# Flush of small numbers by a bit mask made on ScalarE, and words loaded three chunks ahead

## The chip, the core and the metric

The kernel runs on one core of a Trainium2 chip. The core has five engines that work through queues of their own, each in order: TensorE (PE; its weight loads are PEld), VectorE (DVE), ScalarE (ACT), GpSimd (POOL) and SyncE (SP), which here only issues transfers. 16 DMA engines carry the transfers between the chip's memory and the on-chip buffers. The metric is the device time of one execution, in microseconds, as the median of the runs.

## The reference

Three parts follow each other: attention over q, k, v (4 batches, 8 heads, 768 positions, 64 numbers a head, a local window and a few global positions), a mixture of eight experts with one expert per token, and a gated unit. All inputs are fp32 except the weights of the gated unit, whose scale makes them float64 on the host:

```
a = softmax(scale * q k^T + bias, masked);  x = a v            # attention, 3072 tokens x 512
h = max(xc[mask] @ w1[e], 0);  y[mask] = gate_w * (h @ w2[e])  # expert e, w1 512 x 1024, w2 1024 x 512
out[do_compute] = xc + y
gate = 1 / (1 + exp(-(x @ w_gate)));  val = x @ w_val          # gated unit, 512 x 1536 each
result = (gate * val) @ w_out                                  # w_out 1536 x 512
```

What the change touches is a preparation of the last part: `w_gate`, `w_val` and `w_out` arrive as pairs of 32-bit words of a float64 each, and have to become fp32 before the gated unit can multiply with them.

## The kernel before

**Stages.** Attention runs up to about 250 us, two first tiles of expert 0 up to 293 us, experts 1 to 7 up to 562 us, one tile of overflow up to 582 us, and the gated unit up to the end. The tokens of an expert are gathered from rows in memory (`x_rows`) and scattered back by GpSimd (lines 818 and 863).

**An expert** (`expert`, line 838) has two layers for 256 tokens. The first layer is four steps `mp` of 24 matmuls (line 849), each followed by a Relu on ScalarE (`hT`, line 853) and a call of `hook1`. The second is 16 matmuls (line 868), with a call of `hook2` after every four. The first layer's weights of the next expert are split meanwhile into a high part on ScalarE and a low part on VectorE (`we`, lines 809 and 810, by `split_next`), and the next expert's tokens are transposed (line 832) and split (lines 835 and 836, by `prep_x`). At an expert's end VectorE forms the results (line 862) and GpSimd scatters them in two transfers (line 863), of which the second waits until the first has landed.

**The conversion** (`convert`, line 1353) turns 36 chunks of 128 x 512 float64 numbers into fp32, between the steps of the experts. `load_words` brings the words (tile `cvwg`, four buffers). ScalarE squares the high words read as fp32 (`cvcg`, line 1349). VectorE shifts the high words by three and cuts them (`cvd`, line 1360), sets the top bits (1362), takes the exponent (`cvbg`, 1364) and multiplies the low words by it (1366). GpSimd adds that (1367), turns the square into 0 or 1 by comparing it with a threshold (1369), and multiplies the number by it (1370), which flushes numbers that are too small to zero. A store on ScalarE's queue (`cv_store`, line 788) writes the chunk to memory, from where the gated unit loads it.

**What sets the order.** The generator `conv_steps` (line 947) is cut into two half steps a chunk, and `hook1` and `hook2` of expert e run as many of them as the table `CSE` says: for experts 2 to 6 two in each of the first three calls and one in each of the other five. The instructions of an engine then run in the order in which the code is written (`manual_schedule`), and an instruction that waits holds everything behind it on its engine. In the first half step of chunk n the words of chunk n + 2 are loaded; in the second half the chunk n - 1 is stored and chunk n + 1 is begun.

Of the kernel before, what the change touches and what calls it, by code (L numbers as in the profile page):

```python
# [9 lines left out]
F32 = mybir.dt.float32  # L10
F32R = mybir.dt.float32r
I32 = mybir.dt.int32
U32 = mybir.dt.uint32
AF = mybir.ActivationFunctionType
ALU = mybir.AluOpType
# [3 lines left out]
P = 128  # L19
# [10 lines left out]
NM = F2 // P  # L30
# [31 lines left out]
def _i32(c):  # L62
    return c - (1 << 32) if c >= (1 << 31) else c
# [3 lines left out]
def attention_moe_glu_kernel(  # L67
# [7 lines left out]
    nc = tc.nc  # L75
    n_global, n_local, g_gate, g_val, g_out = [a.bitcast(I32) for a in (n_global, n_local, g_gate, g_val, g_out)]
    cp = ctx.enter_context(tc.tile_pool(name="cp", bufs=1))
# [8 lines left out]
    wg18 = cp.tile([P, NC, 18], F32R, name="wg18")  # L86
    nw = cp.tile([P, 4], I32, name="nw")
    prm = cp.tile([P, 8], F32, name="prm")
    flag = cp.tile([P, 1], I32, name="flag")
    nl, ng = prm[:, 1:2], prm[:, 0:1]  # L90

# [46 lines left out]
    def load_chunk(n, after=None):  # L138

        if n % 8 > 3:  # L140
            pool, tag = (raw_p, "raw") if n < 6 else (web[0], "web")
        else:
            pool, tag = (raw_p if ring_place(n) > 3 else rawb[0]), "raw"
        t = pool.tile([P, 1024], F32, tag=tag, name=f"raw{n}")
        src = chunk_src(n)
        if after is not None:
            after.memset(t[:, 0:1], 0.0)
        nc.sync.dma_start(t if (n % 8) < 4 else t.rearrange("p (a f) -> p a f", a=2), src)
        if n % 8 > 3:
            chunks[n] = t  # L150
        else:
            raw_q[n] = t
# [9 lines left out]
    with ExitStack() as actx:  # L162
# [482 lines left out]
        n = 0  # L645
        step[0] = 0
        while n < NS + LAG + 4 or side or pend or rgen:
            step[0] = n
            if n < NS:
                G, i, pr = steps[n]  # L650
# [87 lines left out]
    cvp = ctx.enter_context(tc.tile_pool(name="cvp", bufs=2))  # L738
# [5 lines left out]
    def cv_src(n):  # L744

        if n < 2 * NM:
            p, gv, hf = n // 4, n // 2 % 2, n % 2
            c = slice(2 * hf, 2 * hf + 2)
            src = (g_gate, g_val)[gv].rearrange("(c p) f -> p c f", p=P)[:, c, p * 4 * P:(p + 1) * 4 * P]
            return src, wd[2 * p + gv][:, c].rearrange("p c m f -> p (c m f)")  # L750
        m = n - 2 * NM
        return g_out[m * P:(m + 1) * P, :], od[m]

    cvw, cvt = {}, {}

    def cv_load(n):
        if n < 3 * NM:
            cvw[n] = load_words(nc, cvp, f"g{n}", cv_src(n)[0])

    cvi = {}  # L760

    def cv_first(n):

        if n < 3 * NM:
            cvt[n] = cvp.tile([P, 512], F32, tag="cvd", name=f"cvd{n}", bufs=3)
            wr = cvw.pop(n)
            cvi[n] = convert(nc, cvp, f"g{n}", wr, cvt[n])
            next(cvi[n])

    wf, ws = {}, {}  # L770

# [14 lines left out]
    def cv_store(n):  # L786
        if n in cvt:
            nc.scalar.dma_start(cv_src(n)[1], cvt.pop(n))


    with ExitStack() as ectx:
# [23 lines left out]
        def gather(key, cols):  # L815
            t = ep.tile([P, 2, DM], F32, tag="xg", name=f"xg{key}", bufs=3)
            for u, c in enumerate(cols):
                nc.gpsimd.indirect_dma_start(
                    t[:, u, :], None, X, IndirectOffsetOnAxis(ap=c, axis=0))
            xgs[key] = t  # L820

        def prep_x(key, nt, half):
            if half == 0:
                xTs[key] = (xep.tile([P, NC, 2 * P], F32R, tag="xeh", name=f"xeh{key}"),
                            xep.tile([P, NC, 2 * P], F32R, tag="xel", name=f"xel{key}"))
            th, tl = xTs[key]
            x = xgs[key]
            pt = ps_g.tile([P, 2, 2 * P], F32, tag="g", name=f"xe{key}_{half}")
            for a in range(2):
                c = 2 * half + a  # L830
                for u in range(nt):
                    nc.tensor.transpose(pt[:, a, u * P:(u + 1) * P], x[:, u, c * P:(c + 1) * P], ident)
            n = nt * P
            sl = slice(2 * half, 2 * half + 2)
            nc.scalar.activation(th[:, sl, :n], pt[:, :, :n], AF.Copy)
            nc.vector.tensor_tensor(tl[:, sl, :n], pt[:, :, :n], th[:, sl, :n].bitcast(F32), ALU.subtract)  # L836
# [98 lines left out]
        def loads():  # L935
            while nload[0] < 8 * NE + 8 and not hold[0] and free(nload[0]):
                load_chunk(nload[0])
                nload[0] += 1
# [6 lines left out]
                loads()  # L945

        def conv_steps():
            cv_first(0)
            for n in range(3 * NM):
                cv_load(n + 2)  # L950
                next(cvi[n])
                yield
                cv_store(n - 1)
                cv_first(n + 1)
                run(cvi.pop(n))
                yield
            cv_store(3 * NM - 1)

        conv = conv_steps()

        col = lambda t, n: t[:, n:n + 1]
# [18 lines left out]
        def at_a(what):  # L980
            if what == ("product", NC0):
                rt.counts(pr)
                run(rt.ranks(B - 1, pr, Bm))
                run(rt.weights(B - 1))
            if what == ("product", NPA):
                rt.places(px, Bm, 0, NS_)
                rt.static_rows(px, idx, scratch[0])
                gather("0b", [col(idx, NE)])
                gather(1, cols(idx, 1))
                rt.weight_rows(B - 1)  # L990

                load_chunk(8, nc.gpsimd)
                nload[0], hold[0] = 9, False
                loads()
                cv_load(0)
                cv_load(1)
            if what == ("hidden", 1):
                next(ov)
            if what == ("out", 3):
                prep_x("0b", 1, 0)  # L1000
                prep_x("0b", 1, 1)
                rt.places(pq, Bm, NS_, 3 * NS_)
                rt.static_weights(pq, prob_s, scratch[0])

        def at_b(what):
# [8 lines left out]
            if what[0] == "out":  # L1014
                loads()

        expert_tile("0a", 0, pcol0, col(idx, 0), at_a)
        expert_tile("0b", 0, col(prob_s, NE), col(idx, NE), at_b)

# [50 lines left out]
    with ExitStack() as gctx:  # L1070
# [7 lines left out]
        V, A, G = nc.vector, nc.scalar, nc.gpsimd  # L1078
# [217 lines left out]
        n = 0  # L1296
        for s in range(NSTEP):
            g, pk = divmod(s, NM)
# [38 lines left out]
def load_words(nc, pool, key, src):  # L1337
    wr = pool.tile([P, 1024], I32, tag="cvw", name=f"cvw{key}", bufs=4)
    if len(src.shape) == 3:
        nc.sync.dma_start(wr.rearrange("p (a n) -> p a n", a=src.shape[1]), src)  # L1340
    else:
        nc.sync.dma_start(wr, src)
    return wr


def squares(nc, pool, key, wr):

    c = pool.tile([P, 512], F32, tag="cvc", name=f"cvc{key}")
    nc.scalar.activation(c, wr.bitcast(F32).rearrange("p (n w) -> p n w", w=2)[:, :, 1], AF.Square)  # L1349
    return c  # L1350


def convert(nc, pool, key, wr, dst):

    V, G = nc.vector, nc.gpsimd
    lo = wr.bitcast(U32).rearrange("p (n w) -> p n w", w=2)[:, :, 0]
    hi = wr.rearrange("p (n w) -> p n w", w=2)[:, :, 1]
    c = squares(nc, pool, key, wr)

    V.tensor_scalar(dst.bitcast(I32), hi, 3, 0x3FFFFFF8, ALU.logical_shift_left, ALU.bitwise_and)  # L1360
    yield
    V.scalar_tensor_tensor(dst.bitcast(I32), hi, _i32(0xC0000000), dst.bitcast(I32), ALU.bitwise_and, ALU.bitwise_or)
    b = pool.tile([P, 512], F32, tag="cvb", name=f"cvb{key}")
    V.tensor_scalar(b.bitcast(I32), dst.bitcast(I32), _i32(0xFF800000), None, ALU.bitwise_and)
    yield
    V.scalar_tensor_tensor(b, lo, 2.0 ** -52, b, ALU.mult, ALU.mult)
    G.tensor_tensor(dst, dst, b, ALU.add)

    G.tensor_scalar(c, c, (2.0 ** -15 * 1.125) ** 2, None, ALU.is_ge)
    G.tensor_tensor(dst, dst, c, ALU.mult)  # L1370


class Route:
# [243 lines left out]
def run(*steps):  # L1617
    for g in steps:
        for _ in g:
            pass  # L1620
# [185 lines left out]
```

## Time and profile before

| | us |
|---|---|
| median of 3 runs (1156.45 to 1164.44) | 1156.73 |
| profiled execution | 1158.71 |
| its span | 1157.0 |

The rows further below come from that one profiled execution. Times are microseconds from the start of the span, unless ns is said. L863 is line 863 of the kernel. A matmul's or a copy's row reads: output <- inputs, sizes, and how often. "Idle before" is how long the engine had nothing to run, and the name behind the arrow is what ended it. The granted clock of TensorE (PEclk) is 1.00 at full speed; the mean of the whole execution is 0.963.

### The profile page before, as it was taken

What the parts mean: (1) busy time and instruction counts of PE and PEld (TensorE: products, weight loads), DVE (VectorE), ACT (ScalarE), POOL (GpSimd) and SP (SyncE); (2) the same over time, 40 slices, a digit from 0 to 9 for tenths busy, and PEclk for the clock granted to TensorE, in tenths of its full rate; (3) what the DMA queues carried; (4) which work ended last, traced back from release to release, by engine and by line L of the source; (5) the groups of instructions that cost most, each with busy time, mean ns of one, the idle gap of its engine ahead of it and who ended that gap; (6) DMA issues with size and microseconds to landing.
All of it is one profiled execution on the core that took longest, in us unless ns stands there. A gap on an engine that the chain in (4) does not pass through costs nothing. (4 is left out here: it accounts for less than half of the span.)

```text
span 1157.0 us, 16882 instructions
## 1 busy us (share of the span) xinstructions
PE 1057.2 (91%) x5602; PEld 858.9 (74%) x5602; DVE 805.3 (70%) x1657; ACT 529.2 (46%) x963; POOL 600.3 (52%) x595
## 2 busy tenths in 40 slices
PE   7999999889987687686789999999999999999998
PEld 7999999876755365355458888878888878888886
DVE  6778888866566456645488777777767785877753
ACT  5897888653213213222354343454343364434333
POOL 6655656632477776977754555313544531455410
PEclk8999999999998988898999999999999999999999
DMA  9565555426886477557232225442324252323243
GB/s 172 130 159 132 137 132 134 132 76 211 328 290 231 149 293 277 187 219 271 96 116 91 73 90 193 145 146 91 119 73 164 92 200 92 127 73 99 84 143 130
DMA packets 150242, 176.37 MB, mean 152 GB/s; under 512 B 84224, under 2 KB 94208, under 8 KB 150144
## 3 DMA queue, kind: packets, MB, share of 16 engines
q1 hardware_dynamic: 142240, 156.81, 43.7%
q10 hardware_dynamic: 5184, 9.44, 2.1%
q0 software_dynamic: 2720, 8.92, 2.1%
q8 instruction: 48, 0.79, 0.3%
q14 instruction: 50, 0.41, 0.1%
HBM read 133.45 MB, written 36.18 MB: 147 GB/s over the span
## 5 line engine op out<-in xcount | busy, mean ns | idle before, releaser
L1231 PE MATMUL p<-B,wsp 128*128 128x512 f32 x1512 | 364.6, 391 | 4.7 <-DVE cp L1237 2.6
L1231 PEld LDWEIGHTS p<-B,wsp 128*128 128x128 f32 x1512 | 283.6, 188 | 68.6 <-DVE cp L1237 4.4
L1237 DVE TENSOR_TENSOR cp<-p,cp 128x512 f32<-128x512 f32 x252 | 167.9, 684 | 88.6 <-PE p L1231 86.1
L1197 PE MATMUL o<-wos,gt 128*128 128x512 f32 x864 | 219.1, 395 | 4.4 <-DVE gt L1187 2.4
L1197 PEld LDWEIGHTS o<-wos,gt 128*128 128x128 f32 x864 | 163.5, 190 | 40.9 <-DVE gt L1187 3.0
L849 PE MATMUL h<-xeh,we 128*128 128x256 f32 x448 | 100.2, 319 | 39.2 <-DVE we L810 27.4
L1180 POOL TENSOR_TENSOR wos<-wo,wos 128x512 fp32r<-128x512 f32 x36 | 62.3, 1730 | 113.0 <-ACT wos L1179 113.0
L784 POOL TENSOR_TENSOR ws<-w 128x256 f32<-128x256 f32 x72 | 53.4, 741 | 129.5 <-DVE wsp L1158 129.5
L868 PE MATMUL y<-raw,hT 128*128 128x512 f32 x224 | 101.7, 597 | 17.3 <-ACT hT L853 17.3
L849 PEld LDWEIGHTS h<-xeh,we 128*128 128x128 f32 x448 | 80.0, 216 | 48.1 <-DVE we L810 31.5
L400 ACT ACTIVATE p<-t,mn 128x256 f32<-128x256 f32 (+1 forms) x192 | 83.6, 484 | 36.5 <-DVE mn L391 35.9
L1349 ACT ACTIVATE cvcg<-cvwg 128x512 f32<-128x512 f32 x36 | 24.2, 673 | 159.6 <-POOL cvd L1370 159.6
L1244 ACT ACTIVATE sg<-cp 128x512 f32<-128x512 f32 x72 | 45.2, 632 | 112.7 <-DVE cp L1237 112.0
L278 POOL TENSOR_TENSOR ks<-ring,ks 128x384 fp32r<-128x384 f32 x56 | 56.2, 1025 | 61.8 <-DVE ks L277 45.9
L868 PEld LDWEIGHTS y<-raw,hT 128*128 128x128 f32 x224 | 40.4, 190 | 64.1 <-issue 40.7
L1186 ACT ACTIVATE gt<-gm 128x512 fp32r<-128x512 f32 x36 | 22.8, 632 | 141.5 <-DVE gm L1251 141.5
L391 DVE CUSTOM_DVE_ANT_0 t<-s,far 128x256 f32<-128x256 f32 (+1 forms) x192 | 69.0, 397 | 20.5 <-PE s L366 16.7
L366 PE MATMUL s<-ks,qs 128*128 128x256 f32 (+1 forms) x384 | 69.4, 300 | 5.1 <-POOL ks L278 2.7
L849 PE MATMUL h<-xel,we 128*128 128x256 f32 x224 | 69.6, 311 | 2.1 <-DVE xel L836 2.0
L438 PE MATMUL o<-v,pts 128*128 128x65 f32 x384 | 70.4, 275 | 1.1 <-issue 1.1
L1247 POOL TENSOR_TENSOR gm<-cp,sg 128x512 f32<-128x512 f32 x36 | 54.4, 1510 | 30.3 <-DVE cp L1237 30.3
L1360 DVE TENSOR_SCALAR cvd<-cvwg 128x512 int32<-128x512 int32 x36 | 20.3, 564 | 69.0 <-DMA wd<-cvd 31.8
(274 smaller groups left out, 2061.0 us busy)
## 6 DMA issues: line engine op xcount, KB each, us to landing
raw<-in_moe_w_dram SPq DMA_DIRECT2D x68, 512.0 KB, 6.6
w<-wd SPq DMA_DIRECT2D x36, 512.0 KB, 4.6
wo<-od SPq DMA_DIRECT2D x72, 256.0 KB, 3.0
hd<-gm SPq DMA_DIRECT2D x36, 256.0 KB, 2.0
hf<-hd SPq DMA_DIRECT2D x36, 256.0 KB, 3.4
qraw<-in_q_dram SPq DMA_DIRECT2D x32, 192.0 KB, 3.3
kraw<-in_k_dram SPq DMA_DIRECT2D x32, 192.0 KB, 3.6
v<-in_v_dram SPq DMA_DIRECT2D x8, 768.0 KB, 6.3
```

What stands on the lines that cost most here:

```text
L278: nc.gpsimd.tensor_tensor(dst[:, 1], kk[:, a], dst[:, 0].bitcast(F32), ALU.subtract)
L366: nc.tensor.matmul(st[:, a, c0:256], qt[:, a, i * P:(i + 1) * P], kt[:, a, e, k0:(i + 1) * P], start=(e == 0), stop=(e == 1))
L391: nc.vector.tensor_tensor_reduce(o, i0, i1, 2.0 ** -(h0 + 1), 3.0e38, ALU.add, ALU.min, mn[:, a:a + 1])
L400: nc.scalar.activation(p[:, a, c0:], t[:, a, c0:], AF.Exp, bias=mn[:, a:a + 1], scale=-1.0)
L438: nc.tensor.matmul(o[:, hh, :], t[:, a, 1, :], vt[:, hh, i, :], start=(i == 0), stop=True)
L849: nc.tensor.matmul(ph[:, a, :n], chunks[cb + c][:, wl, m * P:(m + 1) * P], xx[:, c, :n], start=(s_ == 0), stop=(s_ == len(seq) - 1))
L868: nc.tensor.matmul(ys[u], hh[:, f % 2, u * P:(u + 1) * P], w[:, (f % 2) * DM:(f % 2 + 1) * DM], start=(f == 0), stop=(f == NF - 1))
L1180: (V if h else G).tensor_tensor(t[:, 1], src, t[:, 0].bitcast(F32), ALU.subtract)
L1197: nc.tensor.matmul(o[u], gt[:, hl, u * P:(u + 1) * P], w[:, wl, :], start=(m == 0 and i == 0), stop=(m == NM - 1 and i == 2))
L1231: nc.tensor.matmul(ps, lhs, Bt[k][:, xl, c], start=i == 0, stop=i == len(seq) - 1)
L1237: V.tensor_tensor(into, ps, t, ALU.add)
L1247: G.tensor_tensor(t, src, sgs.pop((b, h)), ALU.mult)
```

## The change

Three things are changed, in the conversion alone.

- ScalarE makes the flush: after the square come a Sign of the square less a threshold (a column `thr`, set by one memset at the start) and a Relu scaled by just under 2. Where the number is kept, the result's bits are 0x3FFFFFFF; where it is flushed they are 0. VectorE's shift of the high words now takes that as the mask of its bitwise and, in place of the constant, so the exponent taken from it is zero too and the low words add nothing. GpSimd's comparison and multiplication (lines 1369 and 1370) are gone; its addition stays.
- The half steps are cut in another place. The first of chunk n now holds the shift and the top bits, the second the exponent, the low words and GpSimd's addition; the mask of chunk n + 1 is made in the second half of chunk n, behind the store of chunk n - 1.
- The words of chunk n + 3 are loaded in step n, and three chunks ahead of the first step, still into four buffers.

```diff
--- before.py
+++ after.py
@@ -86,6 +86,8 @@
     wg18 = cp.tile([P, NC, 18], F32R, name="wg18")
     nw = cp.tile([P, 4], I32, name="nw")
     prm = cp.tile([P, 8], F32, name="prm")
+    thr = cp.tile([P, 1], F32, name="thr")
+    nc.gpsimd.memset(thr, -(2.0 ** -15 * 1.0625) ** 2)
     flag = cp.tile([P, 1], I32, name="flag")
     nl, ng = prm[:, 1:2], prm[:, 0:1]
 
@@ -757,15 +759,16 @@
         if n < 3 * NM:
             cvw[n] = load_words(nc, cvp, f"g{n}", cv_src(n)[0])
 
-    cvi = {}
-    def cv_first(n):
+    cvk = {}
+    def cv_keep(n):
         if n < 3 * NM:
-            cvt[n] = cvp.tile([P, 512], F32, tag="cvd", name=f"cvd{n}", bufs=3)
-            wr = cvw.pop(n)
-            cvi[n] = convert(nc, cvp, f"g{n}", wr, cvt[n])
-            next(cvi[n])
+            cvk[n] = normal_bits(nc, cvp, f"g{n}", cvw[n], thr)
+    def cv_steps(n):
+        cvt[n] = cvp.tile([P, 512], F32, tag="cvd", name=f"cvd{n}", bufs=3)
+        return convert(nc, cvp, f"g{n}", cvw.pop(n), cvk.pop(n), cvt[n])
 
     wf, ws = {}, {}
 
@@ -945,14 +948,15 @@
                 loads()
 
         def conv_steps():
-            cv_first(0)
+            cv_keep(0)
             for n in range(3 * NM):
-                cv_load(n + 2)
-                next(cvi[n])
+                cv_load(n + 3)
+                it = cv_steps(n)
+                next(it)
                 yield
                 cv_store(n - 1)
-                cv_first(n + 1)
-                run(cvi.pop(n))
+                cv_keep(n + 1)
+                run(it)
                 yield
             cv_store(3 * NM - 1)
 
@@ -992,8 +996,8 @@
                 load_chunk(8, nc.gpsimd)
                 nload[0], hold[0] = 9, False
                 loads()
-                cv_load(0)
-                cv_load(1)
+                for n in range(3):
+                    cv_load(n)
             if what == ("hidden", 1):
                 next(ov)
             if what == ("out", 3):
@@ -1343,31 +1347,30 @@
     return wr
 
 
-def squares(nc, pool, key, wr):
+def normal_bits(nc, pool, key, wr, thr):
 
     c = pool.tile([P, 512], F32, tag="cvc", name=f"cvc{key}")
     nc.scalar.activation(c, wr.bitcast(F32).rearrange("p (n w) -> p n w", w=2)[:, :, 1], AF.Square)
+    nc.scalar.activation(c, c, AF.Sign, bias=thr)
+    nc.scalar.activation(c, c, AF.Relu, scale=2.0 - 2.0 ** -23)
     return c
 
 
-def convert(nc, pool, key, wr, dst):
-    V, G = nc.vector, nc.gpsimd
+def convert(nc, pool, key, wr, keep, dst):
+    V = nc.vector
     lo = wr.bitcast(U32).rearrange("p (n w) -> p n w", w=2)[:, :, 0]
     hi = wr.rearrange("p (n w) -> p n w", w=2)[:, :, 1]
-    c = squares(nc, pool, key, wr)
-    V.tensor_scalar(dst.bitcast(I32), hi, 3, 0x3FFFFFF8, ALU.logical_shift_left, ALU.bitwise_and)
+    V.scalar_tensor_tensor(dst.bitcast(I32), hi, 3, keep.bitcast(I32), ALU.logical_shift_left, ALU.bitwise_and)
+    V.scalar_tensor_tensor(dst.bitcast(I32), hi, _i32(0xC0000000), dst.bitcast(I32), ALU.bitwise_and, ALU.bitwise_or)
     yield
-    V.scalar_tensor_tensor(dst.bitcast(I32), hi, _i32(0xC0000000), dst.bitcast(I32), ALU.bitwise_and, ALU.bitwise_or)
     b = pool.tile([P, 512], F32, tag="cvb", name=f"cvb{key}")
     V.tensor_scalar(b.bitcast(I32), dst.bitcast(I32), _i32(0xFF800000), None, ALU.bitwise_and)
-    yield
     V.scalar_tensor_tensor(b, lo, 2.0 ** -52, b, ALU.mult, ALU.mult)
-    G.tensor_tensor(dst, dst, b, ALU.add)
-    G.tensor_scalar(c, c, (2.0 ** -15 * 1.125) ** 2, None, ALU.is_ge)
-    G.tensor_tensor(dst, dst, c, ALU.mult)
+    nc.gpsimd.tensor_tensor(dst, dst, b, ALU.add)
 
 
 class Route:
```

On ScalarE's queue, here from the first Relu of expert 2 on, with `hT` the hidden layer, `wd` the store of a converted chunk, `cvcg` the square or mask and `we` the weights of expert 3. Before:

```order
L853 ACTIVATE hT_0_7356<-h_0_7331 128x512
L788 DMA wd_6683<-cvd_7280 128x512
L1349 ACTIVATE cvcg_7365<-cvwg_7288 128x512
L853 ACTIVATE hT_1_7397<-h_1_7372 128x512
L788 DMA wd_6684<-cvd_7317 128x512
L1349 ACTIVATE cvcg_7406<-cvwg_7358 128x512
L853 ACTIVATE hT_2_7438<-h_2_7413 128x512
```

With the change:

```order
L856 ACTIVATE hT_0_7360<-h_0_7335 128x512
L791 DMA wd_6685<-cvd_7294 128x512
L1355 ACTIVATE cvcg_7368<-cvwg_7269 128x512
L1356 ACTIVATE cvcg_7368<-cvcg_7368,thr 128x512
L1357 ACTIVATE cvcg_7368<-cvcg_7368 128x512
L856 ACTIVATE hT_1_7401<-h_1_7376 128x512
L791 DMA wd_6686<-cvd_7364 128x512
L1355 ACTIVATE cvcg_7409<-cvwg_7292 128x512
L1356 ACTIVATE cvcg_7409<-cvcg_7409,thr 128x512
L1357 ACTIVATE cvcg_7409<-cvcg_7409 128x512
L856 ACTIVATE hT_2_7442<-h_2_7417 128x512
```

The store still stands ahead of the chunk's first activation and of the next Relu; two activations are added between them.

On GpSimd's queue at the same place in the program, from the two scatters at the end of expert 1 on. Before:

```order
L863 DMA x_rows<-xo_0_7325,idx 3200x512
L863 DMA x_rows<-xo_1_7328,idx 3200x512
L1367 TENSOR_TENSOR cvd_7317<-cvd_7317,cvbg_7361 128x512
L1369 TENSOR_SCALAR cvcg_7318<-cvcg_7318 128x512
L1370 TENSOR_TENSOR cvd_7317<-cvd_7317,cvcg_7318 128x512
L1367 TENSOR_TENSOR cvd_7364<-cvd_7364,cvbg_7402 128x512
L1369 TENSOR_SCALAR cvcg_7365<-cvcg_7365 128x512
L1370 TENSOR_TENSOR cvd_7364<-cvd_7364,cvcg_7365 128x512
```

With the change:

```order
L866 DMA x_rows<-xo_0_7329,idx 3200x512
L866 DMA x_rows<-xo_1_7332,idx 3200x512
L1373 TENSOR_TENSOR cvd_7364<-cvd_7364,cvbg_7372 128x512
L1373 TENSOR_TENSOR cvd_7405<-cvd_7405,cvbg_7413 128x512
L1373 TENSOR_TENSOR cvd_7446<-cvd_7446,cvbg_7454 128x512
L1373 TENSOR_TENSOR cvd_7487<-cvd_7487,cvbg_7515 128x512
```

One operation a chunk is left of three; the first chunk's addition still stands behind the second scatter.

## Rows read from the trace of the kernel before

**Rows 1.** Page: busy times of the engines; chain that ended last: its first piece.

```profile
PE 1057.2 (91%) x5602; PEld 858.9 (74%) x5602; DVE 805.3 (70%) x1657; ACT 529.2 (46%) x963; POOL 600.3 (52%) x595
...
582.64 3.48 PE gx L1107 x30
```

**Rows 2.** Busy times by stretch, experts 1 to 7 (the last row lies before them).

```profile
core 0: us, PE busy (x) PEld busy (x) DVE busy (x) ACT busy (x) POOL busy (x), PEclk, DMA share, GB/s
308.29:340.55 32.26, 26.89 (x138) 18.52 (x137) 22.59 (x28) 9.71 (x14) 21.33 (x15) 1.00 0.82 294
340.55:378.20 37.65, 30.72 (x138) 21.12 (x137) 20.26 (x27) 10.28 (x15) 28.77 (x19) 0.86 0.62 214
378.20:422.46 44.26, 31.28 (x139) 21.40 (x138) 23.38 (x32) 10.86 (x16) 32.05 (x22) 0.85 0.66 242
422.46:460.54 38.08, 30.72 (x139) 20.98 (x138) 21.23 (x28) 10.28 (x15) 28.60 (x19) 0.87 0.64 226
460.54:501.82 41.28, 30.38 (x139) 20.59 (x138) 25.24 (x32) 10.85 (x16) 32.33 (x22) 0.88 0.68 252
501.82:542.39 40.57, 30.51 (x138) 20.78 (x137) 23.13 (x31) 10.18 (x15) 28.96 (x20) 0.87 0.65 234
542.39:561.69 19.30, 14.31 (x38) 6.20 (x37) 9.40 (x13) 4.54 (x8) 18.00 (x13) 1.00 0.15 57
293.70:308.29 14.59, 14.59 (x122) 14.35 (x121) 5.81 (x17) 2.38 (x4) 3.33 (x3) 1.00 1.04 399
```

**Rows 3.** Waits from 280 to 570: who waited for whom, total, times, longest.

```profile
ACT cvcg L1349 <- POOL cvd L1370: 159.6, 32, 14.8
...
PE h L849 <- DVE we L810: 27.4, 16, 3.0
...
POOL x_rows L863 <- DMA x_rows<-xo,idx: 19.0, 3, 7.4
...
PE y L868 <- ACT hT L853: 17.3, 11, 3.2
...
DVE cvd L1360 <- DMA cvwg<-in_moe_w_val_dram: 10.8, 2, 6.1
```

**Rows 4.** Timeline around 382 to 390: start, length, engine, line, idle before.

```profile
382.29 0.98 POOL L863 DMA_INDIRECT x_rows<-xo,idx  x1 [7.38 <-DMA x_rows<-xo,idx]
...
388.13 0.66 ACT L1349 ACTIVATE cvcg<-cvwg 128x512 f32<-128x512 f32 x1 [14.82 <-POOL cvd L1370]
388.69 0.58 ACT L853 ACTIVATE hT<-h 128x512 f32<-128x512 f32 x1
...
389.33 3.70 PE L868 MATMUL y<-raw,hT 128*128 128x512 f32 x8 [3.22 <-ACT hT L853]
```

**Rows 5.** The conversion's instructions by tile: ns of one, min/median/max, first and last start.

```profile
L1349 ACT ACTIVATE cvcg<-cvwg x36: 659/671/712, 306.2 to 556.9; 128x512 f32<-128x512 f32 x36
L1360 DVE TENSOR_SCALAR cvd<-cvwg x36: 403/427/1520, 304.5 to 553.8; 128x512 int32<-128x512 int32 x36
L1362 DVE SCALAR_TENSOR_TENSOR cvd<-cvwg,cvd x36: 671/684/2191, 304.9 to 554.7; 128x512 int32<-128x512 int32 x36
L1364 DVE TENSOR_SCALAR cvbg<-cvd x36: 426/581/1726, 305.7 to 555.5; 128x512 int32<-128x512 int32 x36
L1367 POOL TENSOR_TENSOR cvd<-cvd,cvbg x36: 1267/1282/2185, 307.1 to 561.6; 128x512 f32<-128x512 f32 x36
L1369 POOL TENSOR_SCALAR cvcg<-cvcg x36: 1487/1723/2352, 308.5 to 562.9; 128x512 f32<-128x512 f32 x36
L1370 POOL TENSOR_TENSOR cvd<-cvd,cvcg x36: 1262/1383/1819, 310.1 to 565.4; 128x512 f32<-128x512 f32 x36
```

**Rows 6.** Line 863, the scatters: time from issue to landing.

```profile
DMA to landing us min/median/max: 2.8/4.4/7.7
```

**Rows 7.** Timeline, TensorE in the overflow tile, first wait for a weight split.

```profile
568.14 0.93 PE L891 MATMUL h<-we,xeh 128*128 128x512 f32 x2 [2.96 <-ACT we L809]
```

**Rows 8.** Timeline, GpSimd at the start: its first data.

```profile
7.84 0.41 POOL L290 TENSOR_SCALAR ring<-kraw 128x256 f32<-128x256 f32 x1 [5.84 <-DMA kraw<-in_k_dram]
```

**Rows 9.** Line 1244, the sigmoid of the gated unit: the table load ahead of it.

```profile
L1244 ACT ACT_TABLE_LOAD  x1: 1283/1283/1283, 597.6 to 597.6; - x1
```

## The prediction

> **What bounds the kernel now.** I read the page's busy times first, then the chain that ended last, then the busy times by stretch, and last what waits for what inside the stretch that the change touches. TensorE is busy for 91% of the span, so a change on other engines pays only where TensorE waits or runs slowly. The chain goes no further back than 582.64 us, the start of the gated unit [rows 1]: a branch stands there, and what came before must be read stage by stage.
>
> All 36 chunks are converted between 304 and 567 us, while experts 1 to 7 run. I cut that stretch at the first second-layer matmul (line 868) of each expert. The six intervals last 32.26, 37.65, 44.26, 38.08, 41.28 and 40.57 us, together 234.1, or 39.0 each; the seventh second layer takes 19.30 more [rows 2]. In the first interval TensorE works for 26.89 us at granted clock 1.00 and idles 5.4. In the other five (201.84 us, 40.4 each) it is busy 30.7 on average, idle 9.7, and the clock reads 0.85 to 0.88. The matmuls of an interval are the same each time, so 30.7 - 26.9 = 3.8 us is what the lower clock (1.2 GHz in place of 2.4 for a part of each interval) adds after the stalls. About 13.5 us of each of these five intervals is not matmul work at full speed.
>
> Who makes TensorE wait? It waits for ScalarE's Relu of the hidden layer (17.3 us) and for VectorE's split of the next expert's weights (27.4 us), and ScalarE waits 159.6 us for GpSimd's last conversion step, line 1370 [rows 3]. One case shows how. GpSimd waits 7.38 us until the first scatter of the expert's rows has landed, issues the second scatter at 382.29, and only then converts. ScalarE has stood 14.82 us before the Square of 388.13, since the store of the chunk ahead of it needs GpSimd's result; the Relu at 388.69 was queued behind it, and TensorE stood 3.22 us until 389.33 [rows 4]. So GpSimd paces the loop. In the five intervals it is busy 28.77, 32.05, 28.60, 32.33 and 28.96 us, mean 30.1; the wait for the first scatter adds 19.0 / 3 = 6.3 [rows 2, 3]. That is 36.4 of 40.4 us, and what is left is hand-over between engines.
>
> **The change part by part.** Experts 2 to 6 take eleven half steps each, 5.5 chunks to an interval.
>
> GpSimd loses lines 1369 and 1370, 1.723 + 1.383 = 3.11 us a chunk [rows 5], 17.1 us an interval. It keeps 30.1 - 17.1 = 13.0 of work and the 6.3 of scatter wait: 19.3.
>
> ScalarE gains a Sign and a Relu of 128x512. The trace has no Sign. The nearest row is the Square of the same tile, 0.671 us [rows 5]; it reads every second word, so I take it as an upper price for the plain Relu, while the bias column and the wait on its own predecessor may add to the Sign. I take 1.4 us for both together, 1.2 to 1.7 as bounds: 7.7 an interval. ScalarE's mean of 10.5 [rows 2] becomes 18.2, and about 20 with the store issues.
>
> VectorE changes one operation: the shift of line 1360 (0.427) becomes one with two tensor inputs, for which line 1362, with the same strided words, is the row (0.684) [rows 5]. That is 0.26 x 5.5 = 1.4 an interval on a mean of 22.6: 24.0. Line 1362 also has a case of 2.191, and line 1364 ran 0.426 at best, 0.581 in the median and 1.726 at worst [rows 5]; the long cases lie beside GpSimd operations. The Trainium skill (SBUF — State Buffer, "Who interferes with whom") says that a VectorE operation with two SBUF inputs is blocked for the whole of a GpSimd operation that reads SBUF and started first. That speaks against the new shift; by it alone, an estimate, each could wait for one add of 1.28 us, 7 us an interval. The trace agrees that such cases exist. But the two GpSimd operations that go ran 3.11 us a chunk, so there is less to meet than before: the long cases should get fewer, and I charge nothing beyond 0.684.
>
> Transfers keep their number and size. Share times length gives 23.3, 29.2, 24.4, 28.1 and 26.4 us, mean 26.3 an interval [rows 2].
>
> Hence the floors of an interval: TensorE 26.9, DMA 26.3, VectorE 24.0, ScalarE 20, GpSimd 19.3. TensorE's is the largest, but four resources close together, each issuing in order, do not reach it. The first interval, 32.26, is the nearest row from above: it has the same matmuls, conversions from start to end and a clock of 1.00, with GpSimd at 21.33 us busy [rows 2], more than the 13.0 to come. The middle of 26.9 and 32.3 is 29.6. I take 30.0, because ScalarE's store still stands behind an add that stands behind the second scatter. What is late next is therefore that scatter (landing in 2.8 to 7.7 us [rows 6]), not the conversion. At 30.0 the clock should stay at 1.00, as it did in the first interval in spite of 5.4 us of stalls.
>
> The six intervals give 234.1 - 180.0 = 54.1 us. In the seventh second layer TensorE is busy 14.31 of 19.30 [rows 2]; I leave 15.0: 4.3. In the tile after it TensorE stood 2.96 us for a weight split [rows 7] that ScalarE, held by the store of a chunk, made late: 3.0.
>
> The loads of words move: before, chunk n + 2 was issued in step n, now n + 3, with the same four buffers. The lead grows from three to five half steps, and the 10.8 us that VectorE waited for words [rows 3] should go; its gain is within the 30.0. The price is on SyncE: the load now needs the buffer of chunk n - 1, whose last reader is the last VectorE operation of the half step just before. Behind it in SyncE's queue are the expert weights. Those need a split that stands still later on VectorE, so they lose nothing; if VectorE fell a step behind, they would be late by one step of some 2.5 us. One more half megabyte is also issued before the weights at about 282 us; at the 399 GB/s of the stretch up to 308.29 us that is 1.3 us, but TensorE was busy 14.59 of 14.59 there [rows 2], so the bounds are 0 and 1.3 and I charge 0.4. The memset of the threshold lies at the start of GpSimd, which then idles 5.84 us for its first data [rows 8]: nothing, and 0.1 without that cover.
>
> Sum: 54.1 + 4.3 + 3.0 - 0.4 = 61.0. From the profiled execution (1158.71; its span is 1157.0) that leaves 1097.7. The median of the runs is 1156.73, 2.0 lower, so I predict **1096 us**.
>
> **The rivals.** (a) ScalarE takes GpSimd's place. For it: it is in order, with the store held until the second scatter has gone out, and then 2 us of mask ahead of each Relu and split. Against: it has 10 us an interval to spare. At 34.5 an interval the six give 27.1, the two pieces behind them 5, less 1.3: 1126.
>
> (b) Everything hides under TensorE: 26.9 an interval gives 72.7 + 5.0 + 3.0 = 80.7: 1076. Against it: DMA would have to be busy for 26.3 of 26.9.
>
> (c) The flush was not what held the loop, and the scatter wait holds it as before: half of the 14.82 us of [rows 4] is the 7.38. The intervals stay near 39 and the time within 10 us of before. Against it: the wait is 6.3 of 40.4, the two operations 17.1.
>
> (d) Slower: the Sign is not in the table that ScalarE has loaded, and each chunk switches it twice. The trace has one load, 1.283 us, at the sigmoid [rows 9]. ScalarE's 20 and the 6.3 of hold leave 12.7 us, so this decides from 2.3 us a chunk on; two loads cost 2.57, so an interval of some 40.4 and 1165 us. Against it: ScalarE's order has two table loads in the whole program before, and two in the change, at the same places. The Trainium skill (ScalarE: Activation LUTs, "What ACT_TABLE_LOAD costs") gives about 2.66 us to a switch of sets with the drain behind it; by that, an estimate, it would be 29 us an interval and over 1200. The trace shows the 1.283 of the load; no run here shows the rest.
>
> **How the numbers follow.** The forecast, intervals of 28 to 32.3 us and 1084 to 1109 in all, gets 0.68; (a) 0.17, (b) 0.08, (c) 0.04, (d) 0.03. The range reaches to (b) below and, above, to intervals of 35 us: 24.1 + 4 - 1.3 is 27 us less, 1130. That leaves out some 0.1. One per cent of this kernel is 11.6 us, about what a measurement can tell from no change: faster by more takes the forecast, (a) and (b), less a little of (a)'s far end: 0.92; within it 0.05; slower 0.03.
>
> **What would show it.** Right: six intervals near 30 us at clock 1.00, GpSimd near 13 us busy in each, ScalarE near 18; the waits for line 1370 gone, a smaller one of ScalarE for GpSimd's add left, mostly next to a scatter. Wrong: TensorE still waiting for the hidden Relu with ScalarE busy or held (a); a DMA share near 1 with TensorE waiting for weights; table loads between Sign and Relu (d); intervals near 39 with GpSimd idle (c).

## The result, and the profile after

The changed kernel takes 1112.05 us in the median (four runs, 1108.45 to 1114.38) against 1158.39 for the kernel before beside it: a ratio of 0.959, 95% interval 0.954 to 0.964. Faster, as forecast, and inside the whole range of 1076 to 1130, but 16 us above the 1096 and 3 us above the narrower forecast of 1084 to 1109. The profiled execution took 1108.45 us.

Busy times by stretch of the changed kernel, cut at the same places as [rows 2] (line 868 is 871 now): six intervals, the seventh second layer, and the overflow tile up to the gated unit.

```profile
core 0: us, PE busy (x) PEld busy (x) DVE busy (x) ACT busy (x) POOL busy (x), PEclk, DMA share, GB/s
308.36:338.64 30.28, 27.73 (x138) 19.77 (x137) 23.66 (x32) 16.66 (x24) 10.49 (x9) 0.94 0.86 325
338.64:371.04 32.40, 29.35 (x138) 21.19 (x137) 22.23 (x28) 16.86 (x25) 12.50 (x10) 0.89 0.77 273
371.04:405.77 34.73, 29.40 (x138) 20.83 (x137) 23.70 (x32) 18.74 (x28) 13.79 (x11) 0.90 0.81 292
405.77:434.44 28.67, 26.64 (x138) 18.48 (x137) 22.14 (x28) 16.91 (x25) 10.23 (x8) 1.00 0.77 278
434.44:471.00 36.56, 30.05 (x139) 21.03 (x138) 23.71 (x32) 18.78 (x28) 14.45 (x12) 0.86 0.83 305
471.00:501.76 30.76, 28.12 (x138) 19.95 (x137) 22.23 (x28) 16.89 (x25) 11.27 (x9) 0.94 0.77 282
501.76:516.66 14.90, 14.30 (x38) 6.20 (x37) 10.28 (x15) 9.40 (x15) 4.92 (x4) 1.00 0.24 92
516.66:533.40 16.74, 15.14 (x50) 8.08 (x49) 7.49 (x10) 5.97 (x8) 6.88 (x7) 1.00 0.47 173
```

The six intervals now take 193.4 us, 32.2 each, against 234.1 and 39.0. In the last five GpSimd's work fell from 30.1 to 12.4 us, ScalarE's rose from 10.5 to 17.6. The rest of the kernel is as it was: from the first transposition of the gated unit to the end of the span 573.3 us, against 574.4.

What is left to lose shows in the waits from 280 to 540 (who waited for whom, total us, times, longest):

```profile
DVE cvd L1367 <- ACT cvcg L1357: 54.0, 14, 8.7
...
ACT cvcg L1355 <- POOL cvd L1373: 34.5, 13, 6.7
...
PE h L852 <- DVE we L813: 21.2, 13, 2.9
POOL x_rows L866 <- DMA raw<-in_moe_w_dram: 13.9, 2, 7.3
POOL x_rows L866 <- DMA cvwg<-in_moe_w_out_dram: 13.0, 2, 6.9
POOL x_rows L866 <- DMA x_rows<-xo,idx: 9.3, 2, 6.8
...
ACT cvcg L1355 <- DMA cvwg<-in_moe_w_out_dram: 8.5, 1, 8.5
...
ACT cvcg L1355 <- DMA cvwg<-in_moe_w_gate_dram: 6.4, 1, 6.4
ACT cvcg L1355 <- DMA w<-wd: 6.2, 1, 6.2
```

The 159.6 us of [rows 3] that ScalarE stood for GpSimd are 34.5 under that name, and 55.6 with the last three lines: in each of these a store went out within 0.1 us of the end of GpSimd's addition, and the mask right behind it, so the transfer that is named is not what was waited for. The Relus are no longer late: the 17.3 us of TensorE for the hidden layer are down to under 1. But TensorE still waits 21.2 us for weight splits (27.4 before), and VectorE's shift waits 54.0 us for the mask, up to 8.7 at a time. That wait is new in name, but the shift stood before, too. In the kernel before, from 280 to 570, it waited for its output buffer, until the store of an earlier chunk had landed:

```profile
DVE cvd L1360 <- DMA wd<-cvd: 31.8, 9, 4.8
...
DVE cvd L1360 <- DMA od<-cvd: 20.5, 7, 4.9
```

Line 866 is the scatter. Some of its lines name transfers that have nothing to do with it; these waits stand at the same place in the program and last as long, so they are read here as waits for the first scatter to land.

The timelines of the fifth interval, picked from those of the four engines (start, length, engine, line, idle before), show how these hang together:

```profile
435.27 0.99 POOL L866 DMA_INDIRECT x_rows<-xo,idx  x1 [6.58 <-DMA raw<-in_moe_w_dram]
436.29 2.50 POOL L1373 TENSOR_TENSOR cvd<-cvd,cvbg 128x512 f32<-128x512 f32 x2
...
437.59 0.33 ACTq L791 DMA_DIRECT2D wd<-cvd  x1
438.02 0.69 ACT L1355 ACTIVATE cvcg<-cvwg 128x512 f32<-128x512 f32 x1 [8.54 <-DMA cvwg<-in_moe_w_out_dram]
...
440.15 0.69 DVE L1367 SCALAR_TENSOR_TENSOR cvd<-cvwg,cvcg 128x512 int32<-128x512 int32 x1 [8.67 <-ACT cvcg L1357]
...
452.42 1.09 PE L852 MATMUL h<-xeh,we 128*128 128x256 f32 x2 [1.73 <-DVE we L813]
455.22 0.80 PE L852 MATMUL h<-xeh,we 128*128 128x256 f32 x2 [1.49 <-DVE we L813]
458.76 0.79 PE L852 MATMUL h<-xeh,we 128*128 128x256 f32 x2 [2.53 <-DVE we L813]
```

The second scatter waited 6.58 us for the first. Two additions stood behind it; the store of the first went out at 437.59, as soon as the addition was done, and ScalarE had stood 8.54 us for it. VectorE had stood 8.67 us for the mask behind that store. From there ScalarE and VectorE work without much rest, yet the weight splits come late by up to 2.5 us each, and TensorE's clock falls to 0.86 in this interval.

### The profile page after: what moved, and what is told of

Same layout as the page of the kernel before. It is cut to its first block, busy times and chain, and to the rows that moved or that the text cites. A ratio compares the mean times of both kernels' runs of the same rounds, so it can differ in the third digit from the quotient of the medians.

```text
span 1106.7 us, 16905 instructions
## 1 busy us (share of the span) xinstructions
PE 1043.5 (94%) x5602; PEld 853.2 (77%) x5602; DVE 806.4 (73%) x1657; ACT 577.2 (52%) x1035; POOL 482.0 (44%) x524
## 4 chain that ended last, share of the span: by engine, by line
PE 45%; DVE 3%; issue 1%; ACT 1%; DMA 1%; another core or an unknown queue 1%; SPq 0%; POOL 0%; ACTq 0%; DVEq 0%
PE p L1235 29%; PE o L1201 15%; DVE cp L1241 1%; DVE B L1128 1%; DMA hf<-hd 1%; DVE gt L1191 1%; DVE t L1132 0%; PE gx L1111 0%; ACT B L1124 0%; DVE ob L1206 0%; ACT wos L1183 0%; ACT gt L1190 0%; ACT wsp L1161 0%; DMA out_dram<-ob 0%
## 5 line engine op out<-in xcount | busy, mean ns | idle before, releaser
L852 PE MATMUL h<-xeh,we 128*128 128x256 f32 x448 | 97.0, 315 | 21.5 <-DVE we L813 21.2
L1190 ACT ACTIVATE gt<-gm 128x512 fp32r<-128x512 f32 x36 | 22.8, 632 | 141.4 <-DVE gm L1255 141.4
L1373 POOL TENSOR_TENSOR cvd<-cvd,cvbg 128x512 f32<-128x512 f32 x36 | 52.3, 1460 | 86.9 <-DVE cvbg L1372 53.6
L393 DVE CUSTOM_DVE_ANT_0 t<-s,far 128x256 f32<-128x256 f32 (+1 forms) x192 | 69.0, 397 | 19.7 <-PE s L368 15.6
L1367 DVE SCALAR_TENSOR_TENSOR cvd<-cvwg,cvcg 128x512 int32<-128x512 int32 x36 | 31.7, 880 | 54.0 <-ACT cvcg L1357 54.0
```

Of the source, the lines that this page charges most:

```text
L393: nc.vector.tensor_tensor_reduce(o, i0, i1, 2.0 ** -(h0 + 1), 3.0e38, ALU.add, ALU.min, mn[:, a:a + 1])
L852: nc.tensor.matmul(ph[:, a, :n], chunks[cb + c][:, wl, m * P:(m + 1) * P], xx[:, c, :n], start=(s_ == 0), stop=(s_ == len(seq) - 1))
```

## The experiments

Theory H (hold) says that this chain, which begins at the second scatter, is what the forecast missed. Rival D blames the DMA engines, rival E the length of ScalarE's own work, rival L the loads of the words. All ratios are to the kernel before, measured on the same chip.

**The two halves of the change.** First the mask with the words two chunks ahead as before:

```diff
-                cv_load(n + 3)
+                cv_load(n + 2)
...
-                for n in range(3):
+                for n in range(2):
```

> The changed kernel with the words loaded two chunks ahead again, as before the change; the mask on ScalarE stays. Theory H (hold): what is left of the stalls comes from one chain: the second scatter of an expert waits 6 to 7 us for the first to land, GpSimd's addition stands behind it, the store on ScalarE's queue waits for the addition, and the masks, Relus and weight splits stand behind the store. The lead of the words has no part in that: 1108 to 1116 us, ratio 0.955 to 0.965, no wait of ScalarE for words over 3 us. Rival L (lead): the third chunk ahead is what made the mask work, since the mask reads the words half a step before the shift did: 1122 us or more, with ScalarE waiting for words several times.

Measured: 1112.14 us, ratio 0.961 (0.956 to 0.966), with six intervals of 193.4 us in all, the same as in the change. The expectation missed in one point: ScalarE does wait for words, six times and 13.6 us in all, two of these over 3 us (3.25 and 3.49). Beside the hold this cost no time. Then the words alone, three ahead in the kernel before:

```diff
-                cv_load(n + 2)
+                cv_load(n + 3)
...
-                cv_load(0)
-                cv_load(1)
+                for n in range(3):
+                    cv_load(n)
```

> The kernel before with the words loaded three chunks ahead and nothing else. H and the prediction: GpSimd still has three operations a chunk and paces the loop, so 1150 to 1160 us, within 1% of before; the 10.8 us that VectorE waited for words may go without any gain. Rival L: a gain of 12 us or more.

Measured: 1155.16 us, ratio 0.996 (0.994 to 0.998). VectorE's wait for words falls from 10.8 us to 1.6, and the whole is some 4 us shorter; ScalarE still stands 150 us for line 1370. So nearly all of the gain is that of the mask together with the new cut of the half steps, which comes with it and which no run separates from it; and rival L falls.

**The second scatter issued later.** Its call is kept and made after the third `hook1` of the next expert, behind the additions of those steps:

```diff
-                nc.gpsimd.indirect_dma_start(
-                    X, IndirectOffsetOnAxis(ap=icols[u], axis=0), xo, None)
+                def scatter():
+                    nc.gpsimd.indirect_dma_start(
+                        X, IndirectOffsetOnAxis(ap=icols[u], axis=0), xo, None)
+                if u and not last:
+                    late.append(scatter)
+                else:
+                    scatter()
...
                 hook1(mp)
+                if mp == 2 and late:
+                    late.pop()()
```

> The changed kernel with the second scatter of each expert issued later: behind the conversion steps of the third first-layer step of the next expert, so that the additions of those steps stand ahead of it on GpSimd. Same work, same transfers. H: the additions no longer wait for the first scatter to land, the stores follow, the waits of VectorE for the mask (54 us in all, up to 8.7 each) mostly go, intervals of 28 to 29.5 us: 1086 to 1098. Rivals D and E: the intervals stay at 32, 1104 to 1114.

Measured: 1083.76 us, ratio 0.935 (0.932 to 0.938). The first six stretches:

```profile
307.86:338.28 30.42, 27.87 (x139) 19.92 (x137) 25.60 (x35) 20.28 (x30) 12.07 (x9) 0.94 0.87 325
338.28:364.40 26.12, 26.12 (x139) 18.36 (x137) 20.39 (x27) 16.07 (x24) 12.81 (x9) 1.00 0.88 313
364.40:393.08 28.68, 26.38 (x139) 18.42 (x137) 23.90 (x32) 18.89 (x28) 14.03 (x10) 1.00 0.93 343
393.08:420.15 27.07, 26.36 (x138) 18.41 (x137) 23.22 (x29) 16.83 (x25) 12.15 (x9) 1.00 0.91 326
420.15:451.21 31.06, 27.98 (x138) 19.81 (x137) 25.07 (x34) 18.86 (x28) 13.44 (x11) 0.95 0.94 354
451.21:477.33 26.12, 26.12 (x138) 18.36 (x137) 23.03 (x29) 16.94 (x26) 11.90 (x8) 1.00 0.89 328
```

The same work and the same transfers, 28 us less, a little more than H allowed for (1086 to 1098): H. The intervals sum to 169.5 us, two of them are TensorE's work and nothing else, and the clock is 1.00 in four of the six. VectorE's wait for the mask is 15.6 us of the 54.0:

```profile
DVE cvd L1375 <- ACT cvcg L1365: 15.6, 12, 3.7
PEld h L852 <- DVE we L813: 9.9, 6, 3.1
```

Rival D falls with it: the DMA engines are busier (0.87 to 0.94) in shorter intervals. Rival E, as the whole cause, falls too, since ScalarE's work is the same.

**The same in the kernel before**, with GpSimd's flush left in.

> The kernel before, flush on GpSimd, with the second scatter of each expert issued later as in the run late_scatter. It tells how much of the loss before was the scatter wait alone. Prediction's theory (GpSimd's work paces the loop: 30.1 us of operations and 6.3 of wait in an interval of 40.4): the wait goes, the 30.1 and the hand-over stay: intervals of 33 to 35, 1122 to 1140 us. Rival S (the scatter wait was all that held the loop, the flush could have stayed): 1084 to 1105. Rival N (no effect before): 1150 or more.

Measured: 1132.00 us, ratio 0.976 (0.972 to 0.979). Two of its intervals:

```profile
373.55:411.13 37.58, 29.76 (x138) 20.64 (x137) 26.36 (x32) 10.89 (x16) 32.51 (x22) 0.86 0.75 266
411.13:445.53 34.40, 29.36 (x139) 20.31 (x138) 23.97 (x28) 10.19 (x15) 29.95 (x21) 0.90 0.72 263
```

And its largest wait from 280 to 570 (line 1378 is 1370 of the kernel before):

```profile
ACT cvcg L1357 <- POOL cvd L1378: 129.7, 32, 6.6
```

GpSimd is busy 32.51 of 37.58 and 29.95 of 34.40, and ScalarE still stands 129.7 us for its last step: with its wait gone, GpSimd's work goes on pacing the loop. The late scatter gives 28 us here and 28 us after the change, and the change gives 46 without and 48 with the late scatter: two holds, one behind the other on GpSimd, each worth the same whether or not the other is there.

**The mask taken away.** The Square, Sign and Relu are left out and the shift has its constant, so numbers that are too small are not flushed:

```diff
-            cvk[n] = normal_bits(nc, cvp, f"g{n}", cvw[n], thr)
+            cvk[n] = None
...
-    V.scalar_tensor_tensor(dst.bitcast(I32), hi, 3, keep.bitcast(I32), ALU.logical_shift_left, ALU.bitwise_and)
+    V.tensor_scalar(dst.bitcast(I32), hi, 3, 0x3FFFFFF8, ALU.logical_shift_left, ALU.bitwise_and)
```

> The changed kernel without the Square, Sign and Relu of the mask; the shift has its constant again, so numbers that are too small are not flushed to zero. ScalarE loses 2.1 us a chunk, some 11 us an interval, and VectorE no longer waits for a mask. The hold of the store behind the second scatter stays. H: the hold still stops ScalarE for the same 6 to 8 us, but less is queued behind it, so the weight splits come some 4 us earlier: intervals of 28.5 to 31, 1090 to 1104 us. Rival E (ScalarE's own work paces the loop): intervals at TensorE's 27 us, 1080 us or less. Rival D (the DMA engines, at a share of 0.77 to 0.86, pace it): no change, 1106 to 1114.

Measured: 1087.35 us, ratio 0.941 (0.935 to 0.946). That lies between H (1090 to 1104) and rival E (1080 or less), and its shape is uneven: four intervals lie at 26.1 to 28.1 us and two at 33.28 and 34.27. Without the mask the hold shows in only two of the six. The same with the late scatter:

> The run no_flush (no Square, Sign and Relu, constant mask in the shift, small numbers not flushed) with the second scatter issued late as in late_scatter. Without the late scatter the mask cost 25 us (1112 against 1087). H: the mask costs that only because it stands behind the hold; without the hold ScalarE has room for it, so against late_scatter (1084) at most 8 us are left: 1076 to 1084. Rival E (the mask's 2.1 us a chunk cost the same everywhere): 1058 to 1064.

Measured: 1068.97 us, ratio 0.922 (0.918 to 0.926), between H's bounds (1076 to 1084) and rival E's (1058 to 1064): neither holds as it was put. The mask costs 25 us with the hold and still 15 without it, so the length of ScalarE's work is paid in part. Four of the six intervals:

```profile
361.20:387.32 26.12, 26.12 (x138) 18.36 (x137) 23.57 (x34) 7.37 (x10) 13.84 (x10) 1.00 0.96 353
387.32:413.44 26.12, 26.12 (x138) 18.36 (x137) 21.14 (x29) 7.48 (x10) 12.84 (x9) 1.00 0.99 366
413.44:439.56 26.12, 26.12 (x138) 18.36 (x137) 22.92 (x33) 7.47 (x10) 14.04 (x10) 1.00 0.99 371
439.56:465.69 26.13, 26.13 (x139) 18.37 (x138) 21.52 (x30) 7.48 (x10) 11.59 (x9) 1.00 0.99 373
```

In these TensorE never waits, at a DMA share of 0.96 to 0.99.

**More on ScalarE**: two further copies of the mask in place in each chunk.

```diff
     nc.scalar.activation(c, c, AF.Relu, scale=2.0 - 2.0 ** -23)
+    for _ in range(2):
+        nc.scalar.activation(c, c, AF.Copy)
```

> The changed kernel with two more copies of the mask in place on ScalarE per chunk, 1.2 to 1.3 us a chunk, some 7 us an interval; the second scatter as in the change. ScalarE is then about 24 us busy in an interval of 32. H: what stands behind the hold on ScalarE is on the path to the next expert's weights, so a good part of the 7 us shows in every second interval at least: 1120 to 1135 us. Rival (ScalarE has the slack that its idle time suggests, 32 - 17 us): within 5 us of the change, 1107 to 1117.

Measured: 1124.56 us, ratio 0.971 (0.966 to 0.975), 12.5 us more than the change. The copies take 0.63 us each, 45 us in all, so rather more than a quarter of what is added to ScalarE is paid, although it is idle for almost half of an interval in the change. The slack of its idle time is not there when it is needed.

**The addition on VectorE.**

```diff
-    nc.gpsimd.tensor_tensor(dst, dst, b, ALU.add)
+    V.tensor_tensor(dst, dst, b, ALU.add)
```

> The changed kernel with the addition of line 1373 on VectorE, so that the conversion has nothing on GpSimd; scatters as in the change. VectorE gets 0.69 us a chunk, 3.8 an interval. H: the store waits for VectorE alone and no longer for the second scatter, so ScalarE is not held: 1084 to 1098. Rival V (VectorE's queue, in order in front of the weight splits, is the pace): 1105 to 1120.

Measured: 1079.46 us, ratio 0.932 (0.928 to 0.936), better than expected. Two of its intervals:

```profile
364.15:392.22 28.07, 26.37 (x138) 18.41 (x137) 26.12 (x40) 18.81 (x28) 4.64 (x4) 1.00 0.92 335
392.22:420.19 27.97, 26.37 (x138) 18.41 (x137) 22.97 (x34) 16.76 (x25) 5.26 (x5) 1.00 0.94 341
```

VectorE is busy for 26.12 of 28.07 us and the loop is faster than with the addition on an engine that is mostly idle. With nothing of the conversion behind the scatters, the scatters stay where they are: a second way to the same end confirms H. The run changes more than that, though: the addition itself takes 0.69 us on VectorE for 1.28 on GpSimd, and no shift takes over 0.70 us any more; what these give beside the hold is not separated.

**What is left: the order on VectorE?** The fourth weight split moved directly behind the third, first with the late scatter, then with the addition on VectorE:

```diff
-                split_next()
+                if fq < 3:
+                    split_next()
+                if fq == 2:
+                    split_next()
```

> As the run late_scatter, and the fourth weight split of the next expert is written directly behind the third, ahead of the conversion's half step that stood between them. In late_scatter the stalls that are left (2.9 us at 439.6, 2.6 at 326.5) are TensorE waiting for that fourth split, which stood behind 2.5 us of conversion on VectorE. If VectorE's order is what is left: intervals of 26.1 to 28, 1072 to 1080. If the transfers (DMA share 0.87 to 0.94) are what is left: 1081 to 1087.

> The run add_on_vector with the fourth weight split directly behind the third, as in late_early_split. In add_on_vector the intervals are 26.1 to 28.8 us, and the stalls left (1.6 to 1.9 us) are TensorE waiting for a weight split. If the order on VectorE makes them, 1074 to 1079; if the order only moves them to another split, as in late_early_split against late_scatter (1083 against 1084), 1077 to 1083. Nothing is left for over 8 us: six intervals at 26.1 would be 157 of 166.

Measured: 1082.94 us (0.933, 0.929 to 0.938) and 1080.46 us (0.932, 0.927 to 0.936), so no change from 1083.76 and 1079.46. In the first kernel the waits of TensorE's weight loads for splits fall from 9.9 us to 6.5, but its matmuls take 1.8 us longer in the six intervals. The stalls that are left there lie at earlier splits, as these two show:

```profile
379.69 0.50 PE L852 MATMUL h<-xeh,we 128*128 128x256 f32 x2 [1.58 <-DVE we L813]
381.90 0.79 PE L852 MATMUL h<-xeh,we 128*128 128x256 f32 x2 [1.59 <-DVE we L813]
```

**Or the mask behind the store?** The two lines exchanged, with the late scatter:

```diff
-                cv_store(n - 1)
-                cv_keep(n + 1)
+                cv_keep(n + 1)
+                cv_store(n - 1)
```

> The run late_scatter with two lines exchanged: in the second half step the mask of the next chunk is written ahead of the store of the chunk before, so that on ScalarE the mask is not held by a store that waits for an addition. In late_scatter VectorE still waits 15.6 us for masks and the mask costs 15 us (1084 against 1069 without it). If that cost is the mask standing behind stores, most of it goes: 1070 to 1078. If it is the 2.1 us a chunk in front of the weight splits on ScalarE, the order changes little: 1080 to 1087.

Measured: 1088.43 us, ratio 0.940 (0.936 to 0.944), no faster than 0.935 (0.932 to 0.938). The 15 us of the mask are not its place behind the store.

**The change again**, beside late_no_flush and add_early_split:

> The changed kernel itself, on the same chip as the two runs beside it: 1106 to 1115, as its own result; the intervals again alternate between some 30 and some 35.

Measured: 1111.60 us, ratio 0.958 (0.954 to 0.963), intervals of 30.3, 32.4, 34.9, 30.5, 34.9 and 31.1 us. What the profile above shows is no accident of one execution.

The fastest kernel that still makes the flush is the one with the addition on VectorE, 1079.46 us: 3% below the change and 7% below the kernel before.

## Why the prediction was right, and where it was short

**GpSimd paced the loop, and the two operations were what to take away.** Right. Its work came out at 12.4 us an interval for 13.0, the wait of ScalarE for line 1370 is gone, and before_late_scatter shows GpSimd's work pacing the loop even without the scatter wait. What is left of ScalarE's wait for GpSimd lies mostly next to a scatter, as foretold. Rival (c), the scatter alone, gave 28 us; the change gives 46 to 48.

**The costs of the parts.** Right. The tile's rows of the change:

```profile
L1355 ACT ACTIVATE cvcg<-cvwg x36: 652/676/697, 306.2 to 510.0; 128x512 f32<-128x512 f32 x36
L1356 ACT ACTIVATE cvcg<-cvcg,thr x36: 721/722/727, 306.9 to 510.8; 128x512 f32<-128x512 f32 x36
L1357 ACT ACTIVATE cvcg<-cvcg x36: 629/631/636, 307.7 to 511.5; 128x512 f32<-128x512 f32 x36
L1367 DVE SCALAR_TENSOR_TENSOR cvd<-cvwg,cvcg x36: 674/692/1778, 308.3 to 512.2; 128x512 int32<-128x512 int32 x36
```

Sign and Relu take 1.35 us together for the 1.4 assumed, and ScalarE 17.6 an interval for 18.2. The shift takes 0.692 for 0.684, VectorE 22.8 for 24.0: the conversion's long cases (over 1 us) did get fewer, 14 after 22. The new shift's mean is 0.880, so its long cases cost (0.880 - 0.692) x 36 = 6.8 us in all, about 1 us an interval, where the prediction had charged nothing and had worked out 7 as the most. How they come about shows in two rows of the fifth interval:

```profile
454.17 2.13 POOL L1373 TENSOR_TENSOR cvd<-cvd,cvbg 128x512 f32<-128x512 f32 x1 [3.97 <-DVE cvbg L1372]
...
455.08 1.77 DVE L1367 SCALAR_TENSOR_TENSOR cvd<-cvwg,cvcg 128x512 int32<-128x512 int32 x1
```

Seven of the 36 shifts took 1.17 to 1.78 us; each of them began while an addition of GpSimd was running. The trace agrees here with the Trainium skill (SBUF — State Buffer, "Who interferes with whom"), by which a VectorE operation with two SBUF inputs is blocked by a GpSimd operation that reads SBUF and started first; but it met only these seven shifts. Rival (d) did not come: no table load stands between Sign and Relu. The program's two loads, of 1.283 us each, lie elsewhere; the prediction's "one load" left out the first of them, at line 327 of the kernel before.

**The intervals: the term that was mis-sized.** 30.0 each was taken, 32.2 measured: 40.7 us gained in the profiled execution where the sum has 54.1. The seventh second layer gave 4.4 (4.3), the tile 4.2 (3.0). So the profiled execution came out 10.8 us above the sum's 1097.7. The other 5 of the 16 us lie in the step from it to the median: that was taken to be 2.0 below it and came out 3.6 above. The prediction named what would be late next, the second scatter, with the addition and ScalarE's store behind it, and then charged 0.4 us an interval above the middle of its bounds for it. The runs late_scatter and add_on_vector put it at 28 to 32 us in all, some 4 to 5 an interval. This was part of rival (a), held to be a variant with a chance of 0.17, at a price between the two: 32.2, where the forecast had 30.0 and (a) 34.5. The sign given for (a), TensorE waiting for the hidden Relu, did not come: it waited for the weight splits.

**Two links of that chain were not followed.** The hold goes on from ScalarE to VectorE, since the shift now waits for the mask: 54.0 us. The prediction charged the new operand with 0.26 us of length and nothing of waiting. The 54.0 are no measure of what this costs, since the shift stood 52.3 us for its output buffer before, and in no_flush, without the mask, still 16.7. And "the clock should stay at 1.00" failed: it is 0.86 to 0.94 in five of six intervals. Per interval 3.7 us are idle, and the matmuls take 2.4 longer than in the undisturbed intervals of late_no_flush (28.5 us busy against 26.1), most of it in the intervals with a lower clock.

**"Four resources close together do not reach it" was wrong as a reason.** In late_no_flush five intervals of six take 26.12 or 26.13 us, TensorE's work, with the DMA engines at 0.94 to 0.99. ScalarE has little to do there (7.4 us), but two intervals of late_scatter take 26.12 us as well, with 16 to 17 on ScalarE and up to 23.0 on VectorE. High shares did not keep this loop from its floor; waits across in-order queues did. The floor itself was 26.1 and not 26.9: the hidden layer's matmuls take 12.84 us in the first interval before and 12.07 in the undisturbed third of late_no_flush.

**The words.** Right for the most part: mask_two_ahead shows no effect of the lead on the time beside the mask, three_ahead_alone some 4 us without it. The half megabyte issued earlier, charged with 0.4 us, cost under 0.1: the first interval begins at 308.36 us for 308.29.

**Open:** how much of the gain belongs to the new cut of the half steps alone; and where the last 15 us of the mask come from once the hold is gone. Neither the order of the splits nor the place of the store moved it. What remains as suspects is the mask's 2 us a chunk ahead of the weight splits on ScalarE, the 15.6 us that VectorE still waits for masks, and VectorE's longer conversion; no run separates these.

## What to carry to other kernels

When work is taken off an engine that paces a loop, follow what still stands on its queue behind a wait, and price that wait through every engine that is in order behind it, not only at the first. A little work on an idle engine can cost much if it stands behind something slow there: moving one addition from GpSimd, idle for over half the time, to VectorE, busy for most of it, gave 32 us. Before reordering, ask which instruction waits for the outside (a transfer to land) and put it behind the work that others wait for.

## What the runs showed of the hardware

The transfers carry more than I had thought safe to count on: at a DMA share of 0.99 and 366 to 373 GB/s (three rows of late_no_flush) TensorE did not wait once. And the granted clock of the change fell to 0.86 to 0.94 in intervals with 2.6 to 6.5 us of idle time, once with a single stall of 2.55 us, where in [rows 2] an interval with 5.4 us of idle time in three stalls (1.17, 1.91 and 2.30) had kept 1.00: the sum of the stalls did not tell which it would be. Of VectorE and GpSimd, in the change, the one that began second waited: the operation of line 1368 on VectorE, 0.69 us in the median, took 1.64 or 1.65 seven times, each time beginning while an addition of GpSimd ran; the addition, 1.28 us in the median, took 2.13 or 2.14 five times, each time beginning while a weight split of VectorE ran.
